# The result products of a retention + soft mixture kernel with slot results stationary and combine weights streaming

## The chip, the core and the metric

The kernel runs on one core of one Trainium2 chip. The metric is device microseconds of one execution. Engines are named as in the profile: PE is TensorE (PEld its weight loads), DVE VectorE, ACT ScalarE, POOL GpSimd, SP SyncE, whose queue issues nearly all the DMAs.

## The reference, cut to what matters

```python
def _attn_ref(q, k, v):                      # q, k, v: (8, 8, 576, 64)
    scores = scale * np.matmul(q, k.transpose(0, 1, 3, 2))
    ...                                      # Dmat: gamma_h ** (i - j) for i >= j, else 0
    return np.matmul(scores * Dmat[None], v)

def _moe_ref(x, phi, w1, w2):                # x: (4608, 512), phi: (512, 32)
    logits = x @ phi
    d = softmax(logits, axis=0)              # over the 4608 positions
    slot_input = (d.T @ x).reshape(8, 4, 512)
    for e in range(8):
        slot_out[e] = np.maximum(slot_input[e] @ w1[e], 0.0) @ w2[e]   # 512 -> 1024 -> 512
    c = softmax(logits, axis=1)              # over the 32 slots
    return c @ slot_out.reshape(32, 512)     # (4608, 512)
```

The attention result, with its heads side by side, is `x`. The change touches the last line, `c @ slot_out`.

## The kernel before, in words

The 4608 positions are 36 tiles of 128. A first loop does retention tile by tile and keeps the logits and a running softmax over the positions. Then come the experts' first products (`L572`), and after them the last stage, which is what the change is about.

**Combine weights.** `split_c` and `stack_c` make, for each of nine groups `b` of four tiles (512 positions), a tile `ct[b]` of 128 rows by 4 x 128 positions in type float32r. The 128 rows are 2 x 2 x 32: the 32 slots' weights split in a rounded part and a remainder, each twice. `stack_c` transposes four pieces on PE (`L537`) and copies the bank to SBUF, on DVE (`L543`) or on ACT (`L545`). By name, `ct[b]` lies in the buffers `x`, `gb`, `g` and `acc`.

**Slot results.** `expert_2(k, n)` are the experts' second products (`L627`, tile `pm`): part `k` of the 512 features (`PARTS`: 0 to 256, 256 to 384, 384 to 512) in 16 steps `n` of four products with 32 stationary columns. `slot_out(k, fill)` turns a finished part into the tile `so` (buffer `kt`), 128 rows by 512 features in float32r: a copy on ACT (`L635`), one product with a constant matrix on PE (`L638`), a copy on ACT (`L639`), and a subtraction on DVE that leaves rounded values in rows 0 to 63 and remainders in rows 64 to 127 (`L640`). `fill` is work written between these steps.

**Result products.** `final(k, b)` multiplies the weights of group `b` by part `k` of `so` (`L659`): for each of four tiles of 128 positions the stationary operand is that piece of `ct[b]`, and 256 features (`k` = 0) or 128 features (`k` = 1, 2) of `so` stream. Products fill banks of 128 x 512 in PSUM (`po`, four buffers): two banks for `k` = 0, one for `k` = 1 and 2. `evac` copies the banks in turn on ACT (`L611`) and on DVE (`L613`) into a tile in SBUF, and SP stores it: `k` = 0 one store of 512 KB for each `b` (the first in two halves, `L663`, the others `L667`); `k` = 1 and 2 one of 512 KB for each pair of `b` (`L671`) and 256 KB for the ninth (`L669`).

The order on each engine is the order of the code. In the last stage it is: all of part 0's expert steps; `slot_out(0)`; then `final(0, b)` in turn with `stack_c(b + 2)` and part 1's steps; `slot_out(1)`, with `final(0, 8)` and four steps of part 2 as its fill; pairs of `final(1, b)`, each pair followed by four steps (16 x 4 products in all with the fill) of part 2; `slot_out(2)`, with `final(1, 6)` in its middle and `final(1, 7)`, `final(1, 8)` at its end; and nine `final(2, b)`.

The host function `unpack` puts the stored tiles into the output's order; that is not part of the time.

Of the kernel before, what the change touches and what calls it, by code (L numbers as in the profile page):

```python
# [15 lines left out]
P = 128  # L16
# [6 lines left out]
NG = NT // 4  # L23
# [11 lines left out]
def tile_order():  # L35
    order = []
    for b0 in range(0, B, 2):
        for c in range(NCH):
            order.append((b0, c))
            order.append((b0 + 1, c))  # L40
        order.append((b0, NCH))
    return order
# [3 lines left out]
def retention_softmoe(ctx, tc, tok, phi, wun, cst, gtab, msel, out):  # L46
    nc = tc.nc
# [308 lines left out]
    for t in range(NT):  # L356
# [37 lines left out]
        if late and t:  # L394
            x, y = late.pop(0)
# [26 lines left out]
    def pbank():  # L422
        return ps_o.tile([P, 512], F32, name="po")
# [55 lines left out]
    for i in range(4):  # L479
        nc.tensor.matmul(pr[i * NS:(i + 1) * NS, 0:1], lhsT=en[:, i * NS:(i + 1) * NS],  # L480
                         rhs=tri[:, 63:64], start=True, stop=True, skip_group_check=True)
# [3 lines left out]
    for z in range(2):  # L485
        for i in range(4):
            nc.tensor.matmul(pph[z][i * NS:(i + 1) * NS, 0:256], lhsT=en[:, i * NS:(i + 1) * NS],
                             rhs=xN[4 * g + i][:, 2 * z:2 * z + 2], start=True, stop=True,
                             skip_group_check=True)
        if z == 0:  # L490
            nc.tensor.matmul(pr[:, P:P + NS], lhsT=lrun.broadcast_to([P, P]), rhs=delta[:, 0:NS],
                             start=True, stop=True, skip_group_check=True)
        nc.vector.scalar_tensor_tensor(
            out=acc[:, z * 256:(z + 1) * 256], in0=acc[:, z * 256:(z + 1) * 256], scalar=alpha,
# [26 lines left out]
    ct = {}  # L521
# [44 lines left out]
    for n in range(8):  # L566
        nh, eh, kp = n // 4, n // 2 % 2, n % 2
        for c in range(2):
            for i in range(4):
                w = unit_tile[(0, 4 * eh + i, nh, kp)]  # L570
                w = w[c] if isinstance(w, tuple) else w[:, c * 512:(c + 1) * 512]
                nc.tensor.matmul(p1[nh][i * NS:(i + 1) * NS, :], lhsT=sim[kp][:, c, 4 * eh + i, :],  # L572
                                 rhs=w, start=(n % 4 == 0 and c == 0),
                                 stop=(n % 4 == 3 and c == 1), skip_group_check=True)
            if n == 0 and c == 0:
                slot_in(1)
        for i in range(4 if n != 2 else 0):
            w = unit_tile[(0, 4 * eh + i, nh, kp)]
# [7 lines left out]
        if n == 2:  # L586
# [3 lines left out]
            so = slots.tile([P, 512], F32R, name="kt")  # L590
# [8 lines left out]
        if n in (5, 6):  # L599
            for i in (free[1:3], free[3:6])[n - 5]:  # L600
                x = slots.tile([P, 2, 4, 2, 2, NS], F32R, name=f"ws{i}")
# [7 lines left out]
    def evac(o, i):  # L609
        if ev[0] % 2 == 0:  # L610
            nc.scalar.copy(out=o, in_=i)  # L611
        else:
            nc.vector.tensor_copy(out=o, in_=i)  # L613
        ev[0] += 1
# [29 lines left out]
    def final(k, b):  # L644
        lo, hi = PARTS[k]
        w = hi - lo
        n = 512 // w
        if k == 0 or b % 2 == 0:
            o = stg.pop(0)
            stg.append(o)  # L650
            open_tile[0] = o
        o = open_tile[0]
        if k:
            o = o[:, b % 2 * 512:(b % 2 + 1) * 512]
        ov = o.rearrange("p (c f) -> p c f", c=4)
        for c0 in range(0, 4, n):
            po = pbank().rearrange("p (c f) -> p c f", c=n)
            for c in range(c0, c0 + n):
                nc.tensor.matmul(po[:, c - c0, :], lhsT=ct[b][:, c, :], rhs=so[:, lo:hi],  # L659
                                 start=True, stop=True)  # L660
            evac(ov[:, c0:c0 + n, :], po)
            if k == 0 and b == 0:
                nc.sync.dma_start(  # L663
                    out=out[0, :, c0 * w:(c0 + n) * w].rearrange("p (c f) -> p c f", c=n),
                    in_=ov[:, c0:c0 + n, :])
        if k == 0 and b:
            nc.sync.dma_start(out=out[b], in_=o)  # L667
        if k and b == NG - 1:
            nc.sync.dma_start(out=out[2 * NG - 1, :, (k - 1) * 512:k * 512], in_=o)  # L669
        elif k and b % 2:  # L670
            nc.sync.dma_start(out=out[NG + (k - 1) * 4 + b // 2], in_=open_tile[0])  # L671
# [22 lines left out]
    for b in range(NG - 1):  # L694
        final(0, b)
        if b + 2 < NG:
            stack_c(b + 2, nc.scalar if b % 2 else nc.vector)
        steps(1, STEPS[b])
    slot_out(1, (lambda: final(0, NG - 1), lambda: steps(2, 4)))
    for b in range(6):  # L700
        final(1, b)
        if b % 2:
            steps(2, 4)
# [28 lines left out]
def unpack(o):  # L732
    import numpy as np
    x = np.empty((NG, 4, P, DM), o.dtype)
    x[..., 0:256] = o[0:NG].reshape(NG, P, 4, 256).transpose(0, 2, 1, 3)
    for k in range(2):
        f = slice(256 + k * P, 256 + (k + 1) * P)
        y = o[NG + k * 4:NG + k * 4 + 4].reshape(4, P, 2, 4, P).transpose(0, 2, 3, 1, 4)
        x[0:8, :, :, f] = y.reshape(8, 4, P, P)
        x[8, :, :, f] = o[2 * NG - 1].reshape(P, 2, 4, P)[:, k].transpose(1, 0, 2)  # L740
    o = x.reshape(NT, P, DM)
    y = np.empty((B, S, DM), o.dtype)
    for t, (b, c) in enumerate(tile_order()):
        if c < NCH:
            y[b, c * P:(c + 1) * P] = o[t]
        else:
            y[b:b + 2, NCH * P:] = o[t].reshape(2, 64, DM)
    return y.reshape(B * S, DM)
# [72 lines left out]
```

## Time and profile before

| | us |
|---|---|
| time before, median of 3 runs (lowest to highest) | 234.91 (232.29 to 267.28) |
| the profiled execution, whole | 234.41 |
| its span, first to last instruction | 232.6 |
| last stage: first result product to the end of the span | 201.9 to 232.6 |
| stores: 18 tiles, 9.44 MB | issued 203.08 to 227.22 |
| last result product starts / last copy of a bank starts | 225.5 / 225.86 |

A row of a timeline has the start, the length, engine, line, operation, and how many instructions were merged; the bracket is idle time of the engine ahead of it and what ended it. A row of instructions by line has the tile names out<-in, the shapes, the count, the busy time and the mean length of one. PE's lengths overlap, since products are pipelined: the pace of a run of products is read from the starts of two rows, not from their lengths. A row of windows has, for a stretch of the span, the busy time of each engine, the granted clock of TensorE, the busy share of the 16 DMA engines and GB/s.

### The profile page before, as it was taken

The page shows a single profiled execution, that of the slowest core. Times are in us where ns is not written, and L with a number is a line of the kernel's source. Part 1 is how long each engine was busy: PE and PEld are TensorE (multiplying, and loading weights), DVE is VectorE, ACT ScalarE, POOL GpSimd, SP SyncE. Part 2 cuts the span into 40 slices and gives each one's busy share as a digit, 9 for nine tenths or more (in the row PEclk, how much of TensorE's full clock was granted, in tenths as well). Part 3 has the DMA queues.
Part 4 walks back from the last instruction along what each step waited for, and adds up shares of the span by engine and source line. Part 5 has one row for each costly group of instructions (what it writes and reads, how often), then busy time and mean ns, then how long its engine had stood idle before and what let it go on. Part 6 is the DMA issues. An engine that isn't in the chain of part 4 may idle for free.

```text
span 232.6 us, 9432 instructions
## 1 busy us (share of the span) xinstructions
PE 218.5 (94%) x4137; PEld 166.6 (72%) x4137; DVE 131.4 (57%) x303; ACT 82.8 (36%) x200; POOL 62.5 (27%) x72
## 2 busy tenths in 40 slices
PE   8789999999999999999998999999899999999980
PEld 7678868868777887787876786888573335788870
DVE  0456637866646766846854774765654232376270
ACT  2232532452433443442343154245130133374350
POOL 2743513515312433412433342332020110000000
PEclk9999999999999999999999999999999999999995
DMA  6999898898799889889879899878491999699777
GB/s 214 405 397 334 315 352 295 279 362 333 259 321 340 293 306 372 320 299 367 267 256 356 288 371 347 274 281 305 154 319 54 343 413 405 253 360 402 276 303 287
DMA packets 23656, 72.56 MB, mean 312 GB/s; under 512 B 2624, under 2 KB 3008, under 8 KB 23616
## 3 DMA queue, kind: packets, MB, share of 16 engines
q1 hardware_dynamic: 23328, 71.51, 84.0%
q8 instruction: 32, 0.52, 0.9%
q10 hardware_dynamic: 288, 0.46, 0.6%
q14 instruction: 8, 0.07, 0.1%
HBM read 62.52 MB, written 9.44 MB: 309 GB/s over the span
## 4 chain that ended last, share of the span: by engine, by line
PE 88%; DVE 4%; DMA 3%; issue 1%; SPq 1%; ACT 0%; DVEq 0%
PE px L234 14%; PE pss L195 12%; PE pn L263 8%; PE pst L255 7%; PE px L222 7%; PE pn L180 7%; PE pm L627 7%; PE po L659 6%; PE pm L277 4%; PE pm L325 4%; PE pst L572 3%; PE pn L572 3%; DMA kv<-in_tok 3%; DVE sT L200 2%; DVE sT L203 1%
## 5 line engine op out<-in xcount | busy, mean ns | idle before, releaser
L155 POOL TENSOR_TENSOR kv<-kv,cst 128x512 f32<-128x512 f32 x36 | 37.5, 1043 | 87.2 <-DMA kv<-in_tok 50.2
L241 DVE TENSOR_TENSOR x<-px,gb 128x512 f32<-128x512 f32 (+1 forms) x37 | 24.9, 675 | 31.3 <-PE px L234 31.2
L234 PE MATMUL px<-sT,kv 128*64 128x128 f32 x576 | 38.6, 276 | 2.7 <-DVE sT L203 1.9
L200 DVE TENSOR_TENSOR sT<-pss,cst 64x256 f32<-64x256 f32 x72 | 30.3, 421 | 12.3 <-PE pss L195 10.0
L181 ACT COPY kt<-pn 128x512 f32<-128x512 f32 x36 | 21.1, 587 | 41.6 <-PE pn L180 41.6
L234 PEld LDWEIGHTS px<-sT,kv 128*64 128x64 f32 x576 | 30.9, 137 | 4.8 <-PE pst L255 2.0
L195 PE MATMUL pss<-qs,kt 64*64 64x64 f32 (+1 forms) x1152 | 32.4, 248 | 1.5 <-issue 0.9
L265 ACT COPY x<-pn 128x512 f32<-128x512 f32 x33 | 19.3, 585 | 38.5 <-PE pn L263 38.4
L195 PEld LDWEIGHTS pss<-qs,kt 64*64 64x64 f32 x1152 | 26.4, 134 | 8.2 <-issue 5.8
L255 PEld LDWEIGHTS pst<-kv 128*64 128x64 f32 x512 | 17.5, 137 | 10.1 <-issue 8.4
L180 PE MATMUL pn<-ident,kv 128*128 128x128 f32 x144 | 22.7, 280 | 0.6 <-DMA kv<-in_tok 0.6
L203 DVE TENSOR_TENSOR sT<-pss,cst 128x512 f32<-128x512 f32 x32 | 22.1, 692 | 0.9
L255 PE MATMUL pst<-kv 128*64 128x64 f32 x512 | 21.9, 228 | 0.0
L263 PE MATMUL pn<-ident,x 128*128 128x128 f32 x132 | 21.7, 287 | 0.1
L222 PE MATMUL px<-qs,sb 64*64 64x128 f32 (+1 forms) x512 | 19.1, 268 | 0.8 <-issue 0.8
L163 POOL TENSOR_TENSOR gb<-g,cst 128x512 f32<-128x512 f32 x16 | 16.6, 1040 | 11.2 <-DVE x L241 11.2
L180 PEld LDWEIGHTS pn<-ident,kv 128*128 128x128 f32 x144 | 15.9, 141 | 2.2 <-DMA kv<-in_tok 0.7
L613 DVE COPY ws<-po 128x512 f32<-128x512 f32 x18 | 12.4, 689 | 8.4 <-PE po L659 8.3
L263 PEld LDWEIGHTS pn<-ident,x 128*128 128x128 f32 x132 | 13.8, 140 | 4.5 <-issue 2.8
L222 PEld LDWEIGHTS px<-qs,sb 64*64 64x64 f32 x512 | 12.6, 133 | 5.6 <-DVE sT L200 3.4
L258 ACT COPY sb<-pst 128x256 f32<-128x256 f32 x32 | 11.7, 367 | 12.7 <-PE pst L255 12.2
L611 ACT COPY ws<-po 128x512 f32<-128x512 f32 x18 | 10.6, 586 | 10.9 <-PE po L659 10.9
(153 smaller groups left out, 233.0 us busy)
## 6 DMA issues: line engine op xcount, KB each, us to landing
ws<-in_w SPq DMA_DIRECT2D x57, 512.0 KB, 6.0
kv<-in_tok SPq DMA_DIRECT2D x35, 512.0 KB, 5.7
qs<-in_tok SPq DMA_DIRECT2D x36, 256.0 KB, 4.6
out<-ws SPq DMA_DIRECT2D x16, 512.0 KB, 3.8
kv<-in_w SPq DMA_DIRECT2D x4, 512.0 KB, 5.5
out<-ws SPq DMA_DIRECT2D x4, 256.0 KB, 2.7
kv<-in_tok SPq DMA_DIRECT2D x2, 256.0 KB, 4.4
qs<-in_w SPq DMA_DIRECT2D x2, 256.0 KB, 6.2
```

The lines of the kernel that those rows point to most:

```text
L155: nc.gpsimd.tensor_tensor(out=v, in0=v, in1=vt[:, c, :].unsqueeze(2).broadcast_to([P, H, D]), op=ALU.mult)
L180: nc.tensor.transpose(pk[:, a, :], k[:, 2 * a:2 * a + 2, :].rearrange("p j d -> p (j d)"), ident)
L181: nc.scalar.copy(out=kt, in_=pk)
L195: nc.tensor.matmul(ps[r, j, a, cols], lhsT=kt[e, a, r], rhs=q[e, a, cols], start=True, stop=True, skip_group_check=True)
L200: nc.vector.tensor_tensor(out=s[r, :, aa, 0:64], in0=ps[r, :, aa, 0:64], in1=tri[r].unsqueeze(1).unsqueeze(2).broadcast_to([D, 2, 2, 64]), ...
L203: nc.vector.tensor_tensor(out=s[:, :, :, 64:P], in0=ps[:, :, :, 64:P], in1=gm.unsqueeze(1).broadcast_to([P, 2, NP, 64]), op=ALU.mult)
L222: nc.tensor.matmul(px[r, j, a // 2, cols], lhsT=sb[i if c == NCH else b % 2][e, a, :], rhs=qT(t)[e, a, cols], start=(i == 0 and a < 2), st ...
L234: nc.tensor.matmul(px[al * D:(al + 1) * D, j, z, :], lhsT=v[:, 2 * a + j, :], rhs=s[:, j, a, :], start=(c == 0 and z == 0), stop=True, ski ...
L241: nc.vector.tensor_tensor(out=xv[:, j], in0=px[:, j, 0:2], in1=g[:, j], op=ALU.mult)
L255: nc.tensor.matmul(pst[j * D:(j + 1) * D, a, :], lhsT=k[:, 2 * a + j, :], rhs=v[:, 2 * a + j, :], start=(c == 0 and a == 0 and b % 2 == 0) ...
L263: nc.tensor.transpose(pn[:, a, :], xT[t][:, a, :], ident)
L265: nc.scalar.copy(out=x, in_=pn)
```

## The change

The operands of the result product change places. For each 128 features of part `k`, that piece of `so` is the stationary operand, and all 512 positions of `ct[b]` stream. A bank then holds 128 features by 512 positions instead of 4 x (128 positions by 128 features) or 2 x (128 positions by 256 features). `unpack` on the host transposes accordingly. The copies of the banks and the stores keep their shapes, sizes and order.

```diff
     def final(k, b):
         lo, hi = PARTS[k]
         w = hi - lo
-        n = 512 // w
         ...
-        ov = o.rearrange("p (c f) -> p c f", c=4)
-        for c0 in range(0, 4, n):
-            po = pbank().rearrange("p (c f) -> p c f", c=n)
-            for c in range(c0, c0 + n):
-                nc.tensor.matmul(po[:, c - c0, :], lhsT=ct[b][:, c, :], rhs=so[:, lo:hi],
-                                 start=True, stop=True)
-            evac(ov[:, c0:c0 + n, :], po)
+        for i in range(w // P):
+            x = slice(i * 512, (i + 1) * 512)
+            po = pbank()
+            nc.tensor.matmul(po, lhsT=so[:, lo + i * P:lo + (i + 1) * P],
+                             rhs=ct[b].rearrange("p a i -> p (a i)"), start=True, stop=True)
+            evac(o[:, x], po)
             if k == 0 and b == 0:
-                nc.sync.dma_start(
-                    out=out[0, :, c0 * w:(c0 + n) * w].rearrange("p (c f) -> p c f", c=n),
-                    in_=ov[:, c0:c0 + n, :])
+                nc.sync.dma_start(out=out[0, :, x], in_=o[:, x])
```

PE's order at the start of part 0's result products (`po<-kt,x`: result product with `so` in `kt` and the group's weights in `x`; `pn<-gb,ws` and `po<-gb,ws`: the transposes of `stack_c`; `pm<-ws,kv`: expert steps):

```order
-L659 MATMUL po<-kt,x 128x256 x4
+L657 MATMUL po<-x,kt 128x512 x2
 L537 MATMUL pn<-gb_2960,ws_3075 128x128 x4
-L659 MATMUL po<-kt,x 128x256 x4
+L657 MATMUL po<-x,kt 128x512 x2
 L537 MATMUL po<-gb_2960,ws_3075 128x128 x4
 L627 MATMUL pm<-ws_102,kv_3023 32x128 x4
 L627 MATMUL pm<-ws_103,kv_3023 32x128 x4
```

Each `final(0, b)` goes from four products of 256 columns to two of 512, at the same place; nothing moves past anything.

PE's order in part 1's pairs and around `slot_out(2)` (`pn<-qs,qs` is its product with the constant matrix):

```order
-L659 MATMUL po<-kt,x 128x128 x8
+L657 MATMUL po<-x,kt 128x512 x2
 L627 MATMUL pm<-ws_108,ws_112 32x128 x4
 L627 MATMUL pm<-ws_109,ws_112 32x128 x4
 L627 MATMUL pm<-ws_110,ws_112 32x128 x4
 L627 MATMUL pm<-ws_111,ws_112 32x128 x4
-L659 MATMUL po<-kt,gb_3028 128x128 x4
+L657 MATMUL po<-gb_3028,kt 128x512
 L638 MATMUL pn<-qs_3072,qs_2694 128x128
```

A pair goes from eight products to two, and the single `final(1, 6)` ahead of `L638` from four to one. DVE, ACT and SP have the same rows in the same order as before.

More of the change, by code (lines that the diff above doesn't have):

```diff
@@ L734, in unpack @@
     x = np.empty((NG, 4, P, DM), o.dtype)
-    x[..., 0:256] = o[0:NG].reshape(NG, P, 4, 256).transpose(0, 2, 1, 3)
+    x[..., 0:256] = o[0:NG].reshape(NG, P, 2, 4, P).transpose(0, 3, 4, 2, 1).reshape(NG, 4, P, 256)
     for k in range(2):
         f = slice(256 + k * P, 256 + (k + 1) * P)
-        y = o[NG + k * 4:NG + k * 4 + 4].reshape(4, P, 2, 4, P).transpose(0, 2, 3, 1, 4)
+        y = o[NG + k * 4:NG + k * 4 + 4].reshape(4, P, 2, 4, P).transpose(0, 2, 3, 4, 1)
         x[0:8, :, :, f] = y.reshape(8, 4, P, P)
-        x[8, :, :, f] = o[2 * NG - 1].reshape(P, 2, 4, P)[:, k].transpose(1, 0, 2)
+        x[8, :, :, f] = o[2 * NG - 1].reshape(P, 2, 4, P)[:, k].transpose(1, 2, 0)
     o = x.reshape(NT, P, DM)
```

## The prediction

> **What bounds the kernel now.** The page's chain, followed back from the last instruction, gives PE nearly all of the span:
>
> ```profile
> PE 88%; DVE 4%; DMA 3%; issue 1%; SPq 1%; ACT 0%; DVEq 0%
> ```
>
> That is a sum over the whole kernel; the change touches only the last stage. There I read the end first: when the last transfer ends, and whether the stores ran without a break. By windows (PE, PEld, DVE, ACT, POOL busy, then clock, DMA share, GB/s):
>
> ```profile
> 204.00:206.00 2.00, 2.00 (x32) 1.80 (x20) 1.50 (x3) 1.32 (x3) 0.00 (x0) 1.00 0.96 362
> 206.00:215.50 9.50, 9.43 (x173) 8.08 (x171) 6.42 (x11) 5.30 (x11) 0.00 (x0) 1.00 1.02 401
> 215.50:223.00 7.50, 7.45 (x116) 6.62 (x107) 3.06 (x5) 3.04 (x7) 0.00 (x0) 1.00 0.60 237
> 223.00:231.00 8.00, 2.82 (x26) 2.68 (x24) 2.76 (x4) 2.08 (x4) 0.00 (x0) 0.75 1.00 392
> 231.00:232.60 1.60, 0.00 (x0) 0.00 (x0) 0.00 (x0) 0.00 (x0) 0.00 (x0) 0.50 0.01 4
> ```
>
> The last stage is a race between PE, which makes results, and the DMA engines, which store them at about 400 GB/s. Part 0's stores run full (206 to 215.5), parts 1 and 2 begin starved (60% from 215.5 to 223, PE busy throughout), and the last 8 us are the DMA engines emptying a backlog while PE has long finished. So the end is the last store, and what sets it is how late the starved stretch lets the backlog start. SP's queue shows where that is (start, length, count):
>
> ```profile
> 213.24 0.33 SPq L667 DMA_DIRECT2D out<-ws  x1
> 215.51 7.14 SPq L671 DMA_DIRECT2D out<-ws  x4
> 222.32 0.33 SPq L671 DMA_DIRECT2D out<-ws  x1
> 222.74 0.38 SPq L669 DMA_DIRECT2D out<-ws  x1
> ...
> 227.22 1.15 SPq L669 DMA_DIRECT2D out<-ws  x1
> ...
> SPq L671 <- DVE ws L613: 7.5, 4, 2.3
> ```
>
> The fourth store of part 1 is issued at 222.32. From it on the stores still to come are five of 512 KB and two of 256 KB, 3.15 MB: the 8 us at 392 GB/s after 223. Everything issued after it comes sooner than the DMA engines can take it. **The time moves with the issue of this store**, which waits for DVE's copy (last row), and that for PE.
>
> What can be won is bounded by the starvation: 215.5 to 223 moved 7.5 x 237 = 1.78 MB, 4.4 us of work at 401 GB/s, so 3.1 us idle; 204 to 206 lost another 0.2. The cap is **3.3 us**.
>
> **The change: one product.** A result product streams 512 columns now, with 108 products (24 + 12 of 256 columns, 72 of 128) becoming 36. No row of before has a float32r product of 512. By line, shape and mean length of one, in the last stage:
>
> ```profile
> L659 PE MATMUL po<-kt,x 128*128 128x128 f32 x48 | 6.2, 280 | 0.0
> L627 PE MATMUL pm<-ws,kv 128*32 128x128 f32 x128 | 4.3, 276 | 0.0
> L659 PE MATMUL po<-kt,x 128*128 128x256 f32 x24 | 4.4, 303 | 0.0
> L627 PE MATMUL pm<-ws,ws 128*32 128x256 f32 x40 | 2.3, 379 | 0.0
> ...
> L572 PE MATMUL pn<-ws,sT 128*32 128x512 f32 x64 | 7.3, 594 | 0.0
> ```
>
> L627 and L572 are plain float32: 276, 379 and 594 ns for 128, 256 and 512 columns, so 256 more columns cost 215 ns (594 - 379). Its pace says the same: L572's products run four side by side in strips of 32 columns, and
>
> ```profile
> 187.95 3.64 PE L572 MATMUL pn<-ws,sT 128*32 128x512 f32 x32
> 191.41 0.83 PE L627 MATMUL pm<-ws,kv 128*32 128x256 f32 x12
> ```
>
> eight such fours take 3.46 us, 0.43 each. L659 is float32r. With 128 columns it lasts as long as plain float32 with 128 (280 against 276), but with 256 columns hardly longer (303): at 256 it streams a column in half the time. Narrow products therefore gain nothing from float32r, and parts 1 and 2 are all narrow. Their pace:
>
> ```profile
> 221.59 2.90 PE L659 MATMUL po<-kt,x 128*128 128x128 f32 x24
> 224.32 0.61 PE L659 MATMUL po<-kt,gb 128*128 128x128 f32 x4
> ```
>
> 2.73 us for 24, 0.114 us each. A product of 512 is bounded below by that 0.114 (the columns cost nothing more) and above by plain float32's 0.43. I take **0.215**, twice the step of a 256-column product, that is half of 0.43: the float32r row of 256 columns is the nearest. It would last about 0.38 us from start to result, as plain float32 with 256 does.
>
> The Trainium skill, "TensorE: Matmul & The Clock Gate", section "Back-to-back issue gap", gives a sustained pace of about 131 ns at 512 columns for streams of load and product, next to an isolated 216. By 131 PE's part below would come to 4.6 us, more than the cap lets through, and the kernel would take 231.1 us. No run here shows a stream of such products yet.
>
> **Part 0, nine groups.** Starts on PE, the first two groups:
>
> ```profile
> 201.93 0.74 PE L659 MATMUL po<-kt,x 128*128 128x256 f32 x4
> 202.50 0.46 PE L537 MATMUL pn<-gb,ws 128*128 128x128 f32 x4
> 202.79 0.71 PE L659 MATMUL po<-kt,x 128*128 128x256 f32 x4
> 203.34 0.46 PE L537 MATMUL po<-gb,ws 128*128 128x128 f32 x4
> ```
>
> A group takes 0.57 or 0.55, say 0.56. Two products of 512 take 0.43. Nine times 0.13 is **1.2 us** of PE, which is on the path: PE has no idle time in this stretch. It buys nothing at once, since part 0's stores already fill the DMA engines; it brings part 1 forward.
>
> **Part 1, three pairs.**
>
> ```profile
> 213.60 1.11 PE L659 MATMUL po<-kt,x 128*128 128x128 f32 x8
> 214.64 1.08 PE L627 MATMUL pm<-ws,kv 128*32 128x128 f32 x32
> 215.65 1.11 PE L659 MATMUL po<-kt,x 128*128 128x128 f32 x8
> ```
>
> A pair takes 1.04 us: 8 x 0.114 = 0.91 and 0.13 of changing over. I keep the 0.13 (bounds 0 and 0.13): 2 x 0.215 + 0.13 = 0.56, so 0.48 less, three times: **1.4 us**. The 32 expert products stay.
>
> **Through slot_out(2) to the fourth store.**
>
> ```profile
> 219.75 0.66 PE L659 MATMUL po<-kt,gb 128*128 128x128 f32 x4
> 220.25 0.44 PE L638 MATMUL pn<-qs,qs 128*128 128x128 f32 x2
> ...
> 219.89 0.27 ACT L635 COPY qs<-pm 128x128 f32<-128x128 f32 x1 [0.90 <-PE pm L627]
> 220.45 0.59 ACT L611 COPY ws<-po 128x512 f32<-128x512 f32 x1 [0.30 <-PE po L659]
> 220.93 0.27 ACT L639 CAST kt<-pn 128x128 fp32r<-128x128 f32 x1
> ...
> 221.24 0.29 DVE L640 TENSOR_TENSOR kt<-pn,kt 64x128 fp32r<-64x128 f32 x1 [1.70 <-ACT kt L639]
> 221.56 1.41 DVE L613 COPY ws<-po 128x512 f32<-128x512 f32 x2
> ```
>
> The chain is ACT's copy of final(1, 6) (L611), which begins 0.70 after that product's start; behind it in ACT's queue L639; then L640 on DVE; then L613, the copy that the fourth store waits for. With one product of 0.38 us L611 can begin 0.42 after it, 0.28 sooner. But L639 then waits for L638, whose row ends at 220.69, and begins right behind that instead of at 220.93. I count **0.2 us**.
>
> Sum: 1.2 + 1.4 + 0.2 = **2.8 us**, under the cap of 3.3. The fourth store is issued near 219.5 instead of 222.32. The first three stores of part 1 then follow part 0's without a break, and about half a microsecond of starvation is left before the fourth.
>
> **What costs nothing.** Part 2's nine products shrink from about 4 us to 2 and the copies become the pace (DVE 0.7 us for each pair of groups, from the row of two L613 in 1.41), but the DMA engines need 1.3 us for a pair's 512 KB at 401 GB/s, so that is hidden; if it were not, the most it could cost is nothing against before, as the same copies were there. The host's other order in `unpack` is outside the time. Copies and stores keep size and shape: nothing. The weight load of `so` in place of `ct` has the same 128 x 128 shape (row below) and hides under a product now twice as long.
>
> The sum is made against the profiled execution, 234.41 us (span 232.6 and 1.8 outside it): 234.41 - 2.8 = **231.6 us**. The median of the runs shown is 234.91, the lowest 232.29, so one execution alone strays by about 1%.
>
> **Rivals.**
>
> *DVE becomes the bound of part 0.* For two groups DVE has two copies of banks and one of `ct`:
>
> ```profile
> 202.70 0.69 DVE L613 COPY ws<-po 128x512 f32<-128x512 f32 x1 [1.28 <-PE po L659]
> 203.31 0.68 DVE L543 CAST x<-pn 128x512 fp32r<-128x512 f32 x1
> 203.91 0.68 DVE L613 COPY ws<-po 128x512 f32<-128x512 f32 x1
> 205.08 0.69 DVE L613 COPY ws<-po 128x512 f32<-128x512 f32 x1 [0.50 <-PE po L659]
> ```
>
> In a round of 2.38 us (205.08 - 202.70) DVE stands idle for 0.50; the change shortens the round by 0.26. It still fits; if the four banks of `po` make PE wait for DVE, part 0's 1.2 us are lost: 1.6 us, 232.8.
>
> *The weight load stands bare.* Each product has its own load:
>
> ```profile
> L659 PEld LDWEIGHTS po<-kt,x 128*128 128x128 f32 x72 | 8.9, 190 | 1.4 <-issue 1.0 <-DVE kt L640 0.4
> ```
>
> A load of 190 ns against a pace of 114 shows loads lying beside products now. If a load could not start while a full-width product streams, a product would cost 0.215 + 0.114 = 0.33, and 24 of them ahead of the fourth store plus 0.39 of changing over would be 8.3 us against 9 x 0.56 + 3 x 1.04 = 8.2 now: no gain, 234.4. The Trainium skill, same page, section "The mechanism", has this rule: a weight load overlaps a running product only where the two use different groups of rows of the array, and here all use all 128. By it the change gains nothing; the trace's 114 against 190 speaks against it.
>
> *Slower: float32r loses its pace at 512 columns.* If it streams 512 as plain float32 does, at 0.43, part 0 takes 9 x 0.30 longer, 2.7 us, part 1's pairs 3 x 0.05 less, and the chain is unchanged: 2.5 us later, **236.9**. It decides from 0.32 us a product on (24 products + 0.39 = 8.2). For it: at 128 columns float32r does run at plain pace. Against it: the pace improves with width, not the other way.
>
> **Chances.** Forecast (2.0 to 3.3 us less) 0.74; DVE the bound 0.12; bare load 0.06; slower 0.05; 0.03 for none of these. The range: 3.3 off the lowest run, 232.29, gives 229.0; at the top the bare load with the strays of a run, up to 235.3; slower is left out. A measurement of this kernel tells about 2%, 4.7 us, from no change. No case reaches that: the cap is 1.4%. Only strays do: faster 0.13, within 2% 0.83, slower 0.04.
>
> **What would show it.** After: products of 512 last near 380 ns, at a pace of 0.215 (part 0's groups 0.43, pairs about 0.56); the fourth store of part 1 is issued near 219.5; DMA share between 214 and 220 near 1; the last store lands 2.8 us sooner, its backlog still 8 us long; ACT and DVE copies unchanged at 0.59 and 0.69. It is wrong if PE waits for `po` in part 0, if a product takes over 0.3 us, or if the stores run slower once they are closer together.

## The result, and the profile after

| | before | changed |
|---|---|---|
| median of 20 runs, us | 233.04 | 231.56 |
| ratio, 95% interval | | 0.9936 (0.9914 to 0.9959) |
| profiled execution: whole / span, us | 234.41 / 232.6 | 229.79 / 228.0 |
| first result product to the end of the span, us | 30.7 (201.93 to 232.6) | 29.3 (198.68 to 228.0) |

The ratio leaves out executions more than 1.5% above the fastest of their kernel.

The median after, 231.56 us, lies on the forecast 231.6, and the change is faster by 0.6%, which is clear of noise but under the 2% from which a kernel is called faster here. But the gain is 1.5 us, not the 2.8 that was worked out, and it lies outside the 2.0 to 3.3 us that the prediction gave a chance of 0.74. The sum started from a profiled execution of 234.41 us, and the median over 20 runs of the same kernel is 233.04. An execution 1.4 us above the median and a gain that was 1.3 us too large cancelled: that the time was hit is luck.

The profiled spans differ by 4.6 us, and 3.25 of those lie ahead of the first result product, where nothing was changed. The stretch from the first result product to the end is the fair measure: it reads 29.3 us in all four profiles of the changed kernel or of the changed kernel with an addition that costs nothing (two more runs of it, and e5 below), while the 20 whole runs stray from 229.79 to 233.47 us. All experiments are read by this stretch, called **the last stretch** from here.

PE in part 0, the first two groups, of the changed kernel (start, length, ..., count):

```profile
198.68 0.73 PE L657 MATMUL po<-x,kt 128*128 128x512 f32 x2
199.25 0.46 PE L537 MATMUL pn<-gb,ws 128*128 128x128 f32 x4
199.54 0.69 PE L657 MATMUL po<-x,kt 128*128 128x512 f32 x2
200.08 0.45 PE L537 MATMUL po<-gb,ws 128*128 128x128 f32 x4
```

0.57 and 0.54 us a group: what four products of 256 columns took. **Part 0 gained next to nothing.** From 201.93 to 213.60, first result product to first pair of part 1, PE took 11.67 us before; now it takes 11.58 (198.68 to 210.26). A pair of part 1, and the chain through `slot_out(2)` to the fourth store of part 1:

```profile
210.26 0.73 PE L657 MATMUL po<-x,kt 128*128 128x512 f32 x2
210.92 1.08 PE L627 MATMUL pm<-ws,kv 128*32 128x128 f32 x32
...
215.28 0.49 PE L657 MATMUL po<-gb,kt 128*128 128x512 f32 x1
215.74 0.49 PE L638 MATMUL pn<-qs,qs 128*128 128x128 f32 x2
215.98 0.48 PE L657 MATMUL po<-g,kt 128*128 128x512 f32 x1
216.30 0.40 PE L657 MATMUL po<-acc,kt 128*128 128x512 f32 x1
216.95 1.22 PE L657 MATMUL po<-x,kt 128*128 128x512 f32 x4 [0.25 <-DVE kt L640]
...
215.81 0.59 ACT L611 COPY ws<-po 128x512 f32<-128x512 f32 x1
216.30 0.27 ACT L639 CAST kt<-pn 128x128 fp32r<-128x128 f32 x1
...
217.68 0.33 SPq L667 DMA_DIRECT2D out<-ws  x1
```

A pair takes 0.66 us instead of 1.04. From 210.26 to 215.28 PE takes 5.02 us where it took 6.15 (213.60 to 219.75). The fourth store of part 1 is issued at 217.68, 2.40 after that instead of 2.57. 0.09 + 1.13 + 0.17 = 1.39 us, the whole gain of the last stretch. The DMA engines in windows (the first lies as far behind the first result product as the window 206 to 215.5 of before, the second ends 1.25 us sooner, the third is 8 us again), and in three places with gaps:

```profile
202.75:212.25 9.50, 9.44 (x157) 6.89 (x156) 6.39 (x11) 5.25 (x11) 0.00 (x0) 1.00 0.98 385
212.25:218.50 6.25, 5.81 (x78) 3.45 (x77) 3.25 (x6) 3.57 (x8) 0.00 (x0) 1.00 0.78 307
218.50:226.50 8.00, 1.57 (x5) 0.63 (x5) 2.29 (x4) 1.36 (x3) 0.00 (x0) 0.81 1.00 393
...
209.50:210.50 1.00, 1.00 (x33) 0.80 (x25) 0.62 (x2) 0.16 (x1) 0.00 (x0) 1.00 0.65 254
215.25:216.25 1.00, 1.00 (x8) 0.70 (x5) 0.00 (x0) 0.70 (x2) 0.00 (x0) 1.00 0.70 270
217.00:218.50 1.50, 1.31 (x5) 0.77 (x6) 1.50 (x3) 1.11 (x3) 0.00 (x0) 1.00 0.24 96
```

The backlog of 8 us at the end is as before (393 GB/s against 392). Starvation ahead of it fell from 3.1 us to about 1.8 (0.35 + 0.30 + 1.14 in the last three rows), most of it just ahead of the fourth store.

### The profile page after: what moved, and what is told of

It reads as the page before. It is cut to its first block, busy times and chain, and to the rows that moved or that the text cites. A ratio compares the mean times of both kernels' runs of the same rounds, so it can differ in the third digit from the quotient of the medians.

```text
span 228.0 us, 9288 instructions
## 1 busy us (share of the span) xinstructions
PE 214.1 (94%) x4065; PEld 158.9 (70%) x4065; DVE 131.2 (58%) x303; ACT 82.7 (36%) x200; POOL 62.6 (27%) x72
## 4 chain that ended last, share of the span: by engine, by line
PE 88%; DVE 4%; DMA 3%; ACT 1%; issue 1%; SPq 1%; DVEq 0%
PE px L234 15%; PE pss L195 12%; PE pn L263 8%; PE pst L255 8%; PE pn L180 7%; PE px L222 7%; PE pm L627 7%; PE pm L277 5%; PE po L657 4%; PE pm L325 4%; PE pst L572 3%; PE pn L572 3%; DMA kv<-in_tok 3%; DVE sT L200 2%; DVE sT L203 1%; ACT ws L611 1%
## 5 line engine op out<-in xcount | busy, mean ns | idle before, releaser
L611 ACT COPY ws<-po 128x512 f32<-128x512 f32 x18 | 10.4, 587 | 8.7 <-PE po L657 8.6
```

## The experiments

What had to be told apart: which part of the change gains; why narrow products were slow; whether the fourth store sets the end; and what more can be had.

| run | last stretch, us | ratio to before (95%) |
|---|---|---|
| e1, part 0 alone turned round | 30.6 | 0.9982 (0.9951 to 1.0014) |
| e2, parts 1 and 2 alone | 29.4 | 0.9952 (0.9922 to 0.9983) |
| changed kernel again, beside e1 and e2 | 29.3 | 0.991 (0.987 to 0.995) |
| e3, products of 64 columns in parts 1 and 2 | 42.2 | one run, 243.92 us |
| e4, 1.3 us of PE ahead of the fourth store | 30.6 | one run |
| e5, the same behind it | 29.3 | one run |
| e6, final(1, 7) moved up | 28.8 | 0.9864 (0.9826 to 0.9903) |
| e7, last expert steps behind final(1, 7) | 28.8 | 0.9916 (0.9878 to 0.9954) |
| e8, e6 with part 0's groups in pairs | 29.65 | 0.9952 (0.9919 to 0.9985) |
| changed kernel again, beside e8 | 29.3 | 0.9943 (0.9909 to 0.9976) |

**e1 and e2: the two halves of the change.** In `final`, the new loop for one side and the old loop for the other (and `unpack` to match):

```diff
+        if k == 0:       # e1; in e2 the two branches change places
             for i in range(w // P):
                 ...      # the new loop
+        else:
+            ...          # the old loop
```

> Only part 0's products are turned round; parts 1 and 2 are as before the change. My theory now: a 256-column float32r product already streams at full pace (about 0.116 us), so two products of 512 (0.231 each after the first) cost what four of 256 cost. Then part 0's groups keep 0.57 and 0.54 us on PE, the stretch from the first result product to the end of the span stays near 30.7 us as before the change, and the time is within 0.2% of before. Rival: part 0 does save PE time, but the copies on DVE or the four banks take it back; then PE shows waits for banks in part 0 and the groups are still shorter than 0.57.

> Only parts 1 and 2 are turned round; part 0 is as before the change. My theory: the whole gain sits here, three pairs of 1.04 us that become 0.66, plus about 0.2 in the chain through slot_out(2): the stretch from the first result product to the end of the span is 29.3 us as with the whole change, the time 0.6% under before. Rival: half or more of the gain comes from part 0, and this run keeps under 0.7 us of it.

> The changed kernel again, beside the two halves: the stretch from the first result product to the end of the span 29.3 us, the time 0.6% under before, and the span ahead of the first result product straying by up to 3 us from run to run whatever the kernel, since nothing is changed there.

e1 kept 30.6 us and e2 came to 29.4. PE in part 0 of e1, products turned round:

```profile
201.85 0.73 PE L658 MATMUL po<-x,kt 128*128 128x512 f32 x2
202.41 0.47 PE L537 MATMUL pn<-gb,ws 128*128 128x128 f32 x4
202.71 0.69 PE L658 MATMUL po<-x,kt 128*128 128x512 f32 x2
203.24 0.45 PE L537 MATMUL po<-gb,ws 128*128 128x128 f32 x4
```

Again 0.56 and 0.53 a group and no waits, so nothing took a gain back: there was next to none. The times agree in direction, but intervals of 0.3 to 0.4% would not separate the halves by themselves; the last stretch does: 0.1 us from part 0, 1.3 from parts 1 and 2.

**e3: what held the narrow products.**

```diff
-            nc.tensor.matmul(po, lhsT=so[:, lo + i * P:lo + (i + 1) * P],
-                             rhs=ct[b].rearrange("p a i -> p (a i)"), start=True, stop=True)
+            m = 64 if k else 512
+            for c in range(0, 512, m):
+                nc.tensor.matmul(po[:, c:c + m], lhsT=so[:, lo + i * P:lo + (i + 1) * P],
+                                 rhs=ct[b].rearrange("p a i -> p (a i)")[:, c:c + m], ...)
```

> The changed kernel, but in parts 1 and 2 each product of 512 columns is cut into eight of 64 with the same stationary operand, each with its own weight load. It tells what held the 128-column products of before at 0.114 us. Theory: the weight load (a float32r load of 128 x 128 needs about 0.107 us, whatever streams), so products of 64 columns also come every 0.11 us, eight take about 0.88, a pair of part 1 takes about 1.9 us on PE and the time rises by several us. Rival: narrow float32r products stream each column at half pace; then 64 columns come every 0.055 to 0.06 us, eight take about 0.45, a pair about 1.0, as before the change.

PE in part 1 of e3:

```profile
211.47 1.97 PE L659 MATMUL po<-x,kt 128*128 128x64 f32 x16
213.37 1.08 PE L627 MATMUL pm<-ws,kv 128*32 128x128 f32 x32
214.38 1.97 PE L659 MATMUL po<-x,kt 128*128 128x64 f32 x16
```

A pair takes 1.90 us, 0.119 for each product with the changing over, as against 0.114 for 128 columns before. Half the columns cost the same. The rival, a half-pace column, would have given 1.0 us and falls. A float32r product of up to 256 columns costs about 0.11 to 0.12 us here, whatever its width. That it is the weight load fits (in the changed kernel the two loads of a group's start, 0.19 each, are over 0.30 after the first began, so loads come 0.11 apart by themselves), but a fixed minimum for the stream would look the same, and no run parted the two.

```profile
198.68 0.30 PEld L657 LDWEIGHTS po<-x,kt 128*128 128x128 f32 x2 [0.20 <-issue]
```

**e4 and e5: does the fourth store set the end?**

```diff
-    slot_out(2, (lambda: final(1, 6), lambda: [final(1, b) for b in (7, 8)]))
+    slot_out(2, (lambda: (warm(12), final(1, 6)), lambda: [final(1, b) for b in (7, 8)]))   # e4
     for b in range(NG):
         final(2, b)
+        if b == 3:                                                                         # e5
+            warm(12)
```

> The changed kernel with twelve more plain float32 transposes on PE (results unused, about 1.3 us) right before final(1, 6), ahead of the fourth store of part 1. Theory: the end moves with the issue of that store, so the stretch from the first result product to the end of the span grows by about 1.3 us, from 29.3 to 30.6. Rival: the stores have slack or PE's end sets the time; the stretch grows by under 0.5 us.

> The same twelve transposes, but right after final(2, 3), behind the fourth store and inside the backlog of stores. Theory: the stretch from the first result product to the end of the span stays at 29.3 us, within 0.2. Rival, PE's end sets the time: it grows by 1.3 us here as well.

The added rows, first of e4, then of e5:

```profile
216.45 1.53 PE L430 MATMUL pst<-ident 128*128 128x128 f32 x12
217.73 0.48 PE L657 MATMUL po<-gb,kt 128*128 128x512 f32 x1
```

```profile
218.56 1.47 PE L430 MATMUL pst<-ident 128*128 128x128 f32 x12
219.79 0.71 PE L657 MATMUL po<-x,kt 128*128 128x512 f32 x2
```

1.28 us of PE ahead of the store (216.45 to 217.73) made the last stretch 30.57 instead of 29.30 us: 1.27 longer, all of it. Nearly as much (1.23) behind it left the stretch at 29.31, though PE's last product then started 0.74 us later (21.82 us after the first result product instead of 21.08). The store sets the end; PE's end does not. The other profiles agree: in nine of them, before and both halves among them, the span ends 10.29 to 10.32 us after the issue of this store. The exceptions are e3, where PE loses its clock (last section), and e6 and e7, which come next.

**e6 and e7: bringing that store forward.**

```diff
 # e6
-    slot_out(2, (lambda: final(1, 6), lambda: [final(1, b) for b in (7, 8)]))
+    slot_out(2, (lambda: [final(1, b) for b in (6, 7)], lambda: final(1, 8)))
 # e7
-    for b in range(6):
+    for b in range(8):
         final(1, b)
-        if b % 2:
+        if b in (1, 3, 7):
             steps(2, 4)
-    slot_out(2, (lambda: final(1, 6), lambda: [final(1, b) for b in (7, 8)]))
+    slot_out(2, (lambda: final(1, 8), lambda: None))
```

> The changed kernel with final(1, 7) moved ahead of slot_out(2)'s product with the constant matrix, so that its copy on DVE no longer stands behind the subtraction. Theory: the fourth store of part 1 is issued about 0.8 us sooner, and 0.6 to 0.8 us of the 1.1 us of starvation before it goes; the stretch is 28.6 us, the time 0.2 to 0.4% under the changed kernel. Rival: part 2's first store comes later by as much, and nothing is gained.

> The changed kernel with the last four expert steps of part 2 after final(1, 7) instead of after final(1, 5): pairs 0-1, steps, 2-3, steps, 4-7, steps, and slot_out(2) with final(1, 8) as its only fill. Theory: the fourth store is issued about 1.9 us sooner, the starvation before it goes, and what remains before part 2's first store is about 0.2 us; the stretch is 28.4 us, the time 0.4% under the changed kernel and 1% under before. Rival: the bare chain through slot_out(2), with less work beside it, delays part 2's first store past the end of the backlog, and the gain is under 0.3 us.

The store is issued 18.13 us after the first result product in e6 and 17.06 in e7, against 19.00. Both stretches are 28.8 us, 0.53 shorter: e6 gained 0.2 us less than expected, e7 0.4 less. DMA windows, first of e6, then of e7 around its first store of part 2:

```profile
214.50:215.50 1.00, 1.00 (x20) 0.64 (x10) 0.10 (x1) 0.42 (x2) 0.00 (x0) 1.00 0.68 262
216.50:218.00 1.50, 1.27 (x5) 0.74 (x5) 0.91 (x3) 0.70 (x3) 0.00 (x0) 1.00 0.79 317
```

```profile
219.00:220.00 1.00, 1.00 (x18) 0.53 (x11) 0.29 (x1) 0.37 (x2) 0.00 (x0) 1.00 0.70 266
222.50:223.50 1.00, 1.00 (x4) 0.42 (x3) 1.00 (x3) 0.79 (x2) 0.00 (x0) 1.00 0.71 274
```

Each still starves in these two places for about 0.3 us. In e7 the second gap has moved to part 2's first store, issued 20.12 us after the first result product against 19.91 in the changed kernel: with the fourth store out of the way, the next one holds up the backlog. That is e7's rival, in part.

Neither gap explains why both stretches shrank by only 0.53 us, for the starvation of each is 0.8 to 0.9 us less than the changed kernel's (all three have the gap of 0.35 us in part 0). The rest went at the end. The last half microsecond of the stores, first of the changed kernel, then of e6 and e7:

```profile
225.99:226.49 0.50, 0.00 (x0) 0.00 (x0) 0.00 (x0) 0.00 (x0) 0.00 (x0) 0.50 0.80 299
225.05:225.55 0.50, 0.00 (x0) 0.00 (x0) 0.00 (x0) 0.00 (x0) 0.00 (x0) 0.50 0.12 45
229.11:229.61 0.50, 0.00 (x0) 0.00 (x0) 0.00 (x0) 0.00 (x0) 0.00 (x0) 0.50 0.13 45
```

In the changed kernel the 16 DMA engines finish together; in e6 and e7 one of them is still storing for about 0.3 us when the others are done. Why is not shown. All three traces have two transfers of instructions, each of 16 KB in one packet of 0.9 to 1.0 us, between 9 and 17 us after the first result product. They could leave one engine behind, and the longer starvation of the changed kernel could hide that; no run tested it.

e6 and e7 are the best versions run, and the last stretch doesn't tell them apart. Against before it would give a ratio of 0.992 for both. That is e7's; e6's 0.9864 rests on four executions, and I take the surplus for straying of the stretch ahead.

**e8: part 0's groups in pairs**, to save changing over between kinds of work:

```diff
-    for b in range(NG - 1):
-        final(0, b)
-        if b + 2 < NG:
-            stack_c(b + 2, nc.scalar if b % 2 else nc.vector)
-        steps(1, STEPS[b])
+    for b in range(0, NG - 1, 2):
+        final(0, b)
+        final(0, b + 1)
+        for i in (b, b + 1):
+            if i + 2 < NG:
+                stack_c(i + 2, nc.scalar if i % 2 else nc.vector)
+            steps(1, STEPS[i])
```

> The kernel of the moved final(1, 7), and besides in part 0 the groups in pairs: final(0, b) and final(0, b + 1) one behind the other, then both stack_c, then the steps. Theory: the first product after other work costs about 0.34 us or 0.30 us instead of 0.23, so four products in a row cost about 1.03 us against 0.57 + 0.54 now, and PE saves 0.08 us a pair and 0.3 us in all ahead of the fourth store; the stretch from the first result product to the end of the span is 28.4 to 28.6 us against 28.77, the time about 0.8% under the changed kernel's. Rival: four banks in a row leave no bank free for the next transposes, PE waits for copies, and the stretch is 28.8 us or more.

> The changed kernel once more, on the same chip as the kernel with the pairs: stretch 29.3 us, time 0.6 to 0.9% under before.

It missed: 29.65 us, 0.9 longer than e6. The saving on PE is there, and so is a new wait:

```profile
201.20 1.20 PE L657 MATMUL po<-x,kt 128*128 128x512 f32 x4
202.24 0.46 PE L537 MATMUL pn<-gb,ws 128*128 128x128 f32 x4
...
203.91 1.21 PE L657 MATMUL po<-x,kt 128*128 128x512 f32 x4 [0.30 <-DVE x L543]
...
212.14 0.70 PE L657 MATMUL po<-acc,kt 128*128 128x512 f32 x2 [0.72 <-DVE acc L543]
...
201.97 1.29 DVE L613 COPY ws<-po 128x512 f32<-128x512 f32 x2 [1.28 <-PE po L657]
203.18 0.68 DVE L543 CAST x<-pn 128x512 fp32r<-128x512 f32 x1
```

Four products in a row take 1.04 us, as expected. But the copy of the next `ct` (L543) now stands on DVE behind two copies of banks (last two rows), and PE waits for it, not for banks as the rival had it. In the order of before PE has no such wait.

## Why the prediction came out as it did, step by step

- **What bounds the kernel: right.** e4 shows that delaying the fourth store of part 1 moves the end by as much, e5 that PE behind it is free. e6 and e7 show the limit: bringing the store forward counts only in part.
- **One product of 512 columns: pace 0.215 forecast, 0.235 measured.** Four in a row (e8) take 1.04 us and two 0.57, so two more cost 0.47. Its row by line has 439 ns on average; the 380 forecast holds for products that follow another (0.40 in the row of 216.30):

```profile
L657 PE MATMUL po<-x,kt 128*128 128x512 f32 x24 | 8.4, 439 | 0.4 <-DVE kt L640 0.3 <-ACT ws L611 0.2
```

- **Narrow products at plain float32's pace for each column: wrong.** 64 columns in e3 cost what 128 and 256 cost before, 0.11 to 0.12 us, so the cost does not depend on the width up to there. The measured 0.114 us that the sum used stands; its reason was another.
- **Part 0: the step that failed.** 1.2 us forecast, 0.09 measured. The 0.56 us of a group of before was read from the starts of two rows and holds about 0.10 for the first product after other work; the 0.43 for the changed group was twice a bare pace and holds none. 2 x 0.235 + 0.10 = 0.57. The four products of before show the same two parts: in its first group they start at 201.93, 202.15, 202.27 and 202.38, so 0.22 us for the first and about 0.115 for each of the others. At 256 columns they already streamed at the pace per column of 512. The prediction's own price says so too: it took 0.215 as twice the step of a 256-column product, and by that four of 256 cost the same 0.43 as two of 512. It kept 0.13 for changing over in part 1 and left it out in part 0.
- **Part 1: right in kind, 1.4 forecast, 1.13 measured.** A pair takes 0.66 instead of 0.56: two products at 0.235, not 0.215, and 0.19 of changing over, not 0.13.
- **Through slot_out(2): 0.2 forecast, 0.17 measured, by another limit.** L611 starts 0.53 us after its product (215.81 after 215.28), not 0.42, because that product follows other work and lasts 0.49. L639 still comes right behind L611 and not, as forecast, behind L638, which ends at 216.23.
- **Starvation left ahead of the fourth store:** half a microsecond forecast, 1.14 measured. The store is issued 19.00 us after the first result product instead of 20.39, so 1.4 us sooner and not 2.8.
- **Part 2 hidden: right.** Copies set its pace (PE waits for ACT in two rows there) and the backlog hid it.
- **DVE as the bound of part 0: did not happen.** Its 1.6 us lie nearest to the gain that was measured, but for another reason: PE has no wait in part 0 of the changed kernel or of e1. e8 shows that DVE's copy becomes the bound when the order changes.
- **The weight load bare: only for the first product of a row of them.** The PEld row above starts with its product, 198.68, and the first product costs about 0.10 more than the rest; that this is its load was read from the rows and not tested. The others came at 0.235, not at the 0.33 that the prediction worked out for a bare load. The Trainium skill's page "TensorE: Matmul & The Clock Gate", section "The mechanism", says that a weight load overlaps a running product only where the two use different groups of rows; this trace disagrees, with loads of 0.19 us and a pace of 0.235. The same page of the Trainium skill has 131 ns as the sustained pace at 512 columns ("Back-to-back issue gap"); the 0.235 us here do not reach it.
- **Slower, plain float32's pace: did not happen**, 0.235 against 0.43.
- **The base.** The 234.41 us of one execution was 1.4 above the median of 20. The forecast named this straying but did not correct for it; it is why the time was hit while the gain was half.

Not settled is why the stretch ahead of the result products strays by up to 4 us between executions (198.20 to 202.29 us in the profiles here) with the same instructions.

## What to carry to other kernels

When a block of instructions is replaced, cost the old and the new block by the same rule: either both from start to start of their neighbours, or both by a bare pace. Widening the streamed side pays where products are narrower than what their fixed cost covers; here it paid from 128 columns in float32r and brought next to nothing from 256. And where stores run behind compute, find the store from which the queue never runs dry: work added ahead of it counted in full here, and work added behind it not at all. Time saved ahead of it counts until the next limit shows, as in e6 and e7.

## What the runs showed of the hardware that was not expected

**A busy TensorE lost its clock.** In e3, from 220.21 us on PE has hardly anything but 64-column products with a weight load for each, the end of part 1 and then part 2. Their starts are 0.11 us apart without a break up to 223.58, and at 223.66 the granted clock fell to 0.50 though PE had no idle time. In the profiles of before and after it fell only once the last product had started, 1.4 and 3.7 us later. This is one run, and why it happened is open.

```profile
210.00:220.00 10.00, 10.00 (x179) 9.13 (x178) 3.12 (x6) 2.51 (x5) 0.00 (x0) 1.00 0.67 263
220.00:225.00 5.00, 5.00 (x49) 4.80 (x40) 1.40 (x3) 1.60 (x4) 0.00 (x0) 0.87 0.47 184
225.00:230.00 5.00, 5.00 (x25) 5.00 (x25) 0.97 (x2) 0.88 (x2) 0.00 (x0) 0.50 0.48 187
```

A product then took 0.213 us (24 from 227.78 to 232.90), nearly twice its time in part 1, and the last stretch became 42.2 us:

```profile
227.78 5.31 PE L659 MATMUL po<-x,kt 128*128 128x64 f32 x24
232.90 0.40 PE L659 MATMUL po<-gb,kt 128*128 128x64 f32 x1
```

**Issuing one store took three times as long.** In the changed kernel the issue of the store of `final(0, 7)` took 1.00 us where it took 0.33 before, and the DMA engines starved 0.35 us right behind it (the window from 209.50 above). First before, then the changed kernel:

```profile
212.25 0.33 SPq L667 DMA_DIRECT2D out<-ws  x1
208.91 1.00 SPq L663 DMA_DIRECT2D out<-ws  x1
```

It comes back in every run with part 0 turned round (0.89 to 1.02 us) and not in e2 (0.33). It costs nothing here, since it lies ahead of the starvation before the fourth store. The number of stores under way doesn't explain it: three had not landed yet at this issue before, and two in the changed kernel. Why is open.
